# Moving the residual of two row blocks from TensorE to VectorE, and reordering the steps around it, in a fused retention and Fourier-mixing kernel

## The chip, the cores and the metric

The kernel runs on one core of a Trainium2 chip. A core has five engines that run their own instruction streams side by side and wait for one another through semaphores: TensorE (PE in the profile) multiplies matrices, VectorE (DVE) and ScalarE (ACT) do elementwise work and read TensorE's results out of PSUM, GpSimd (POOL) does elementwise work in SBUF and issues some transfers, and SyncE (SP) issues the other transfers. The metric is the device time of one execution in microseconds. Before the change it was 242.21 us, the median of three runs that lay between 242.1 and 242.36.

## The reference

The first half is retention, a linear attention with a decaying state, for 4 batches, 8 heads, 768 positions and head size 64. The second half adds a two-dimensional Fourier transform of the result to it, normalises each row and adds a two-layer network:

```python
for t in range(S):
    state = gamma[None, :, None, None] * state + np.einsum('bhd,bhe->bhde', k[:, :, t], v[:, :, t])
    y[:, :, t] = scale * np.einsum('bhd,bhde->bhe', q[:, :, t], state)
x = y.transpose(0, 2, 1, 3).reshape(B, S, H * D)
X = np.fft.fft(np.fft.fft(x, axis=1), axis=2)
u = x + np.real(X)
un = (u - u.mean(-1)) / np.sqrt(u.var(-1) + 1e-06)
out = u + np.maximum(un @ w_ch1, 0.0) @ w_ch2
```

The weights w_ch1 and w_ch2 have 512 x 2048 and 2048 x 512 elements. Inputs and output are float32.

## The kernel before, in words

The 768 rows of a batch are six chunks of 128 rows. Retention works on pairs of heads, four to a batch. For each pair q, k and v are loaded, cast to 16 bits (q16, kd, v16) and transposed on TensorE; TensorE then makes the scores of a chunk (wkA), VectorE masks and scales them (atm), TensorE makes the chunk states (wkK), VectorE scans them over the chunks (s), and TensorE adds up the output from both (wkY). ScalarE or VectorE evicts wkY into x, the input of the Fourier part.

The Fourier transform is done as matrix products with tables of cosines and sines: csp and ssp over the positions, cd and sd over the 512 columns. VectorE first folds x onto its sums and differences (xab), a DFT over positions gives g, and a second product with cd and sd gives pq. For column zero there is a small product with csn, a copy of the cosine table in another order, whose results become the per-row number g0. Row blocks 0 to 2 come straight from g; blocks 3 to 5 use a mirrored copy, g16r. Then u is the residual x plus pq plus g0, statistics of u follow (bst, stats), un is u minus its mean in 16 bits, and unT its transpose. The first layer makes psh from unT and the weight w116 (L1104 in batch 0), ht is its evicted positive part, the second layer makes psc from ht and w216 (L1130), and ob is the output.

The four batches are chained in software: while the network of batch b runs on TensorE, the retention of batch b + 1 is mixed in. Batch 0 has nothing before it, so its retention and its Fourier part are a start-up phase written out by hand: the string FIRST names every step in the order in which it is issued, and the function pin ties the steps of each engine to that order. Each engine runs its own steps in that order and waits where an input is missing. After FIRST the function emit sorts the remaining steps by due times, and behind those a scheduler may still move instructions of an engine past each other.

The names in FIRST that matter here have a step, numbers, and an engine after the @ sign (a ScalarE, v VectorE, g GpSimd). For pair i: am i h is the score product of half h (the function am_unit, L522), ae the mask (L536), kv the chunk states (L550), sc the scan (L559), yi and yx the output products (L572, L582), x the eviction (L599 on VectorE, L596 on ScalarE), fs the fold (L760), xs a row sum for the mean (L805). s e c d is a part of the first DFT (L827; e says cosine or sine, c the column half, d the side), and ge its eviction (L837). g0, g1 and g2 are three parts of the column-zero step: a small copy and scaling on VectorE (L874, L882), nine small TensorE products (L891), and two small VectorE steps (L897, L900). sa b p is part p of the second product of block b (L921): part 1 is the residual, two products of an identity with x. ua is the step that writes u (L929, L931), bn its statistics (L953, L954), nh and n write un (L943, L963), pt and pe transpose and evict block 0's un (L975, L981), gr copies one of the four mirrored tables (L863), w issues a weight transfer, csn copies a third of the reordered table (L355).

PSUM results live in rotating buffers: five banks for the products of the start-up (ps_g), and three (ps_pm) for psh and psc. A product that takes a bank waits until its former content has been evicted. In batch 0 the first layer goes block by block: for each of blocks 0, 1 and 2 there are four groups of 16 products (the function h0_unit), evicted in turn by ScalarE (groups 0 and 2, L1111) and VectorE (groups 1 and 3, L1113). Between the last n step and these evictions ScalarE also makes eight mask copies (late_consts, L277), which are tied behind the last n. The mirrored products for blocks 3 to 5 (L1025, L1028) are mixed in between.

The q, k and v of batch 0 are loaded by SP at the start (L215). Two q loads of batch 1 follow directly on SP (L220, L221, issued at L195). The eight weight transfers are issued by GpSimd at their w steps. The next SP loads wait for the seventh weight transfer.

Of the kernel before, what the change touches and what calls it, by code (L numbers as in the profile page):

```python
# [12 lines left out]
ALU = mybir.AluOpType  # L13
# [26 lines left out]
v22@a s010 k30@a t30 e30@a t31 v21@g e31@a ae201@v ta30 ae200@v kv2 ae211@v yi21 ae210@v gk2@g  # L40
sc2 csn2@a w1 csn1@v am30 ae300@v ta31 yi20 yx2 v32@g x20@a ae301@v xs0@v x21@a ta41 fl3@a gk3@g
s100 am31 ae311@v s000 v31@g kv3 fs2 s101 ge10@a ae310@v w2 s001 w3 yi31 sc3 ge00@a yi30 yx3 g0
x30@a sa00 sa10 edge x31@v fs3 w4 gr0 sa11 csn0@v s011 xs2@a xs3@v w5 s111 xs1@a sa20 mean
ge01@a sa02 sa01 ge11@v sa03 nh0@a gr3 sa12 nh1@a gr1 sa13 g1 sa21 pt0 g2 ua1@v pt1 sa22 pe0@a
pe1@a w6 ua0@v bn1 sa23 ua2@a gr2 n1 bn2 n2 w7
"""
# [15 lines left out]
def kernel(  # L62
# [122 lines left out]
    def load_unit(b, i, after=None, names="qkv"):  # L185
        def run():
            h0 = 2 * PAIR_ORDER[i]
            for name in names:
# [7 lines left out]
                if after is not None:  # L196
                    for x in (w_dma[after].ins, lb[0]["mm"].ins):
                        tc.add_manual_dep(dma.ins, x.name,
                                          mybir.DependencyInfo(mybir.DependencyClass.Sync,
                                                               mybir.DependencyReason.DATA),  # L200
                                          reason="loads in turn")
# [16 lines left out]
    for name, i in LOADS0:  # L218
        first_load(name, i, nc.sync)()
    load_unit(1, 0, None, "q")()  # L220
    load_unit(1, 1, None, "q")()  # L221

# [680 lines left out]

    lb = {}

    def sa_unit(kb, part):
        def run():
            if part == 0:
                if 0 not in lb:
                    lb[0] = dict(u=up.tile([P, NCH, DM], f32, tag="u32", name="u32"),  # L910
                                 unT=up.tile([P, 4, S], f16, tag="unT", name="unT"),
                                 st=stt.tile([P, NCH, 4], f32, tag="stats", name="stats"))
                lb[0]["pq", kb] = ps_g.tile([P, DM], f32, tag="g", name="pq0")
# [11 lines left out]
    def ua_unit(kb, eng):  # L925
        def run():
            dst, src, g0 = lb[0]["u"][:, kb], lb[0]["pq", kb], fd[0]["g0"][:, kb:kb + 1]
            if eng == "a":
                nc.scalar.activation(dst, src, AF.Identity, bias=g0, scale=1.0)  # L929
            else:  # L930
                nc.vector.tensor_scalar(out=dst, in0=src, scalar1=g0, scalar2=0.0, op0=ALU.add,  # L931
                                        op1=ALU.add)
        return run
# [162 lines left out]

    def h0_unit(kb, g):
        def run():
            unT = lb[0]["unT"]
            psh = ps_pm.tile([P, 4, P], f32, tag="pm", name="psh0")  # L1100
            for f in range(4):
                fb = 4 * g + f
                for cb in range(4):
                    mm = nc.tensor.matmul(psh[:, f], w116[:, cb, fb * P:(fb + 1) * P],  # L1104
                                          unT[:, cb, kb * P:(kb + 1) * P],
                                          start=(cb == 0), stop=(cb == 3))
# [81 lines left out]
    def first_unit(name):  # L1188
# [17 lines left out]
        if kind == "ge":  # L1206
            return s1e_unit(n[0], n[1], eng or "a")
        if kind == "nh":
            return n0_unit(n[0], eng or "a")
# [34 lines left out]
    def mix_units(b, kbs, s0, s1, u0, u1):  # L1244
        def turn(j):
            def run():
# [6 lines left out]
                ([unT_unit(b, kb) for kb in kbs], u0, u1)]  # L1253

    def emit(streams):
        ev = []
# [19 lines left out]
    for b in range(B):  # L1276
        majors = []
        if b == 0:
            for kb in range(3):
                if kb:  # L1280
                    majors.append(unT_unit(0, kb))
                majors += [h0_unit(kb, g) for g in range(4)]
        else:
            majors += [h_unit(b, 0, fb) for fb in range(NFB)]
# [57 lines left out]
```

## Time and profile before

The profiled execution took 242.18 us, against a median of 242.21; its span, from the first to the last instruction, was 240.4 us.

| Engine | Busy us | Share of the span |
|---|---|---|
| PE (TensorE matmul) | 228.3 | 95% |
| DVE (VectorE) | 173.4 | 72% |
| PE weight loads | 142.5 | 59% |
| ACT (ScalarE) | 120.8 | 50% |
| POOL (GpSimd) | 82.8 | 34% |

The granted TensorE clock was 1.0 over the span. The chain of work that ended last is 85% TensorE, 4% VectorE, 3% transfers. In a row of a timeline the first number is the start in microseconds from the beginning of the span and the second the time from the first start to the last end in that row; then come the engine, the line, the operation, the result and its inputs, the shape, the count, and in brackets the idle time before it with what ended it. Matmuls overlap, so the work of one is better read from the distance between two starts than from its duration.

### The profile page before, as it was taken

The numbers are of one execution on the slowest core, as the hardware profiler recorded it, in microseconds if no ns is written. First come the engines' busy times: TensorE is split into PE (matmuls) and PEld (weight loads), VectorE is DVE, ScalarE is ACT, GpSimd is POOL, SyncE is SP. The second block draws the span as 40 slices with busy tenths as digits, with TensorE's granted clock in tenths as the row PEclk, the third lists the DMA queues.
The fourth block names the chain that finished last, engine by engine and source line by source line (L and its number), as shares of the span: only waits on it lengthen the run. The fifth ranks groups of instructions, "written<-read, shape, count | busy, mean of one in ns | idle before, by whom it ended". The sixth has DMA issues, their size and how long they took to land.

```text
span 240.4 us, 5243 instructions
## 1 busy us (share of the span) xinstructions
PE 228.3 (95%) x1999; PEld 142.5 (59%) x1999; DVE 173.4 (72%) x421; ACT 120.8 (50%) x268; POOL 82.8 (34%) x151
## 2 busy tenths in 40 slices
PE   0988999999999999999999999999999999999994
PEld 0466779766774756665567446655675455446542
DVE  8999887958898789977895749977886557215121
ACT  5989758675864544931148406722366227203400
POOL 7678802675300197840002808920004124000000
PEclk9999999999999999999999999999999999999999
DMA  7999999999999289979999488675100331221012
GB/s 181 231 271 238 236 206 208 215 248 246 260 215 230 47 197 218 179 144 146 256 277 208 103 174 213 131 109 153 46 0 0 90 109 24 43 90 45 0 44 87
DMA packets 100808, 36.77 MB, mean 153 GB/s; under 512 B 91440, under 2 KB 97840, under 8 KB 100784
## 3 DMA queue, kind: packets, MB, share of 16 engines
q1 hardware_dynamic: 96560, 32.25, 63.2%
q0 software_dynamic: 4224, 4.19, 10.5%
q8 instruction: 15, 0.25, 0.5%
q14 instruction: 9, 0.07, 0.1%
HBM read 27.26 MB, written 6.29 MB: 140 GB/s over the span
## 4 chain that ended last, share of the span: by engine, by line
PE 85%; DVE 4%; DMA 3%; POOL 2%; ACT 2%; SPq 1%; issue 1%; ACTq 0%
PE psc L1130 34%; PE psh L1087 28%; PE psh L1104 3%; PE wkA L664 3%; DMA v<-in_v_dram 3%; PE ps L847 3%; PE wkY L718 2%; PE pq L1009 2%; PE ps L827 1%; PE wkY L714 1%; PE wkK L683 1%; PE pq L921 1%; SPq L215 1%; PE tq L620 1%; POOL q16z L453 1%
## 5 line engine op out<-in xcount | busy, mean ns | idle before, releaser
L1130 PE MATMUL psc<-w,ht 128*128 128x512 f16 (+2 forms) x400 | 88.9, 370 | 0.0
L1087 PE MATMUL psh<-unT,w 128*128 128x384 f16 x448 | 81.6, 326 | 0.3 <-ACT ht L1091 0.3
L1130 PEld LDWEIGHTS <-ht 128*128 128x128 f16 x400 | 37.6, 98 | 36.7
L1087 PEld LDWEIGHTS <-w 128*128 128x128 f16 x448 | 42.1, 98 | 24.2 <-issue 0.8
L1091 ACT ACTIVATE ht<-psh 128x384 f16<-128x384 f32 x66 | 31.7, 490 | 41.2 <-PE psh L1087 40.6
L1037 POOL TENSOR_TENSOR u<-u,x 128x256 f32<-128x256 f32 x21 | 13.3, 635 | 107.8 <-DVE u L1016 95.6
L1134 DVE SCALAR_TENSOR_TENSOR ob<-psc,stats,u 128x512 f32<-128x512 f32 (+2 forms) x25 | 18.1, 725 | 29.2 <-PE psc L1130 29.0
L1093 DVE TENSOR_SCALAR ht<-psh 128x384 f16<-128x384 f32 x46 | 25.3, 550 | 8.9 <-PE psh L1087 8.4
L667 DVE TENSOR_TENSOR atm<-wkA,maskp 128x512 f16<-128x512 f32 x36 | 23.6, 681 | 1.5 <-PE wkA L664 1.5
L1051 ACT ACTIVATE un<-u,stats 128x512 f16<-128x512 f32 x21 | 14.9, 719 | 12.2 <-DVE stats L1050 8.2
L1049 DVE BATCH_NORM_STATS2 bst<-u 128x6 f32<-128x512 f32 x21 | 14.5, 688 | 4.9 <-POOL u L1039 4.7
L693 DVE SCALAR_TENSOR_TENSOR s<-s,gk,wkK 128x128 f16<-128x128 f16 x48 | 16.2, 337 | 2.4 <-ACT s L689 1.6
L726 ACT ACTIVATE x<-wkY,gexp 128x384 f16<-128x384 f32 x24 | 12.9, 581 | 9.0 <-PE wkY L718 8.9
L438 POOL TENSOR_SCALAR kd<-k,gexp 128x384 f16<-128x384 f32 x24 | 13.8, 586 | 3.3 <-DMA k<-in_k_dram 3.1
L664 PE MATMUL wkA<-qTz,kT 128*128 128x256 f16 x72 | 13.2, 272 | 0.1
L1039 POOL TENSOR_TENSOR u<-u,x 128x256 f32<-128x256 f32 x21 | 13.3, 635 | 0.0
L1011 ACT COPY qn<-pq 128x128 f32<-128x128 f32 x18 | 4.9, 274 | 13.7 <-PE pq L1009 13.7
L1104 PEld LDWEIGHTS <-w 128*128 128x128 f16 x192 | 11.0, 98 | 0.9 <-issue 0.6
L1104 PE MATMUL psh<-unT,w 128*128 128x128 f16 x192 | 11.4, 219 | 0.1
L1016 DVE SCALAR_TENSOR_TENSOR u<-pq,g,qn 128x256 f32<-128x256 f32 x18 | 8.5, 474 | 3.2 <-PE psh L1087 2.5
L443 POOL TENSOR_SCALAR v<-v 128x768 f16<-128x768 f32 x12 | 10.0, 832 | 1.6 <-DMA v<-in_v_dram 1.6
L664 PEld LDWEIGHTS <-kT 128*128 128x128 f16 x72 | 6.9, 98 | 5.7 <-issue 0.6
(177 smaller groups left out, 311.9 us busy)
## 6 DMA issues: line engine op xcount, KB each, us to landing
q<-in_q_dram SPq DMA_DIRECT2D x16, 384.0 KB, 6.1
k<-in_k_dram SPq DMA_DIRECT2D x16, 384.0 KB, 5.4
v<-in_v_dram SPq DMA_DIRECT2D x16, 384.0 KB, 6.0
out_dram<-ob SPq DMA_DIRECT2D x23, 256.0 KB, 2.4
w<-in_moe_w_ch_dram POOLq DMA_DIRECT2D x8, 512.0 KB, 10.9
unT<-un SPq DMA_TRANSPOSE x15, 2.4
out_dram<-ob SPq DMA_DIRECT2D x1, 192.0 KB, 1.9
kT<-kd SPq DMA_TRANSPOSE x10, 3.0
```

What stands on the lines that cost most here:

```text
L438: kc = nc.gpsimd.tensor_scalar(out=kd[:, :, h2, :], in0=k32[:, h2], scalar1=gkd[:, h0 + h2:h0 + h2 + 1], scalar2=1.0, op0=ALU.mult, op1=AL ...
L664: mm = nc.tensor.matmul(wk[:, c2], st["kT"][:, c, :], st["qT"][:, :, c, :], start=True, stop=True)
L667: nc.vector.tensor_tensor(out=st["atm"][:, 2 * part:2 * part + 2], in0=wk, in1=maskp[:, PAIR_ORDER[i]].unsqueeze(1).to_broadcast([P, 2, 2, ...
L693: nc.vector.scalar_tensor_tensor(out=s16[:, c], in0=s16[:, c - 1], scalar=gk2[:, hp:hp + 1], in1=wk[:, c - c0], op0=ALU.mult, op1=ALU.add)
L1049: nc.vector.bn_stats(bst, u[:, kb, :])
L1051: nc.scalar.activation(un, u[:, kb, :], AF.Identity, bias=stats[:, kb, 0:1], scale=-1.0)
L1087: nc.tensor.matmul(psh, w116[:, cb, fb * P:(fb + 1) * P], unT[:, cb, rt * 384:(rt + 1) * 384], start=(cb == 0), stop=(cb == 3))
L1091: nc.scalar.activation(ht16[:, fb, :], psh, AF.Relu, bias=0.0, scale=-1.0)
L1093: nc.vector.tensor_scalar(out=ht16[:, fb, :], in0=psh, scalar1=-1.0, scalar2=0.0, op0=ALU.mult, op1=ALU.max)
L1104: mm = nc.tensor.matmul(psh[:, f], w116[:, cb, fb * P:(fb + 1) * P], unT[:, cb, kb * P:(kb + 1) * P], start=(cb == 0), stop=(cb == 3))
L1130: nc.tensor.matmul(psc[:, c0:c1], ht16[:, fb, rb3 * P:(rb3 + 1) * P], w216[:, fb, c0:c1], start=(fb == 0), stop=(fb == NFB - 1))
L1134: nc.vector.scalar_tensor_tensor(out=ob[:, c0:c1], in0=psc[:, c0:c1], scalar=lb[b]["st"][:, rb, 3:4], in1=lb[b]["u"][:, rb, c0:c1], op0=AL ...
```

## The change

In the order string, two table copies (csn1, csn0) move from the middle of the fourth pair's attention to behind its scan, and the row sum xs0 moves from there to behind the last fold. The DFT part s100 moves ahead of am30. The small product g1 moves ahead of edge, g2 behind ge11. The residual parts sa11 and sa21 of blocks 1 and 2 are taken out; in their place ua for blocks 1 and 2 adds x on VectorE in two instructions of 256 columns each, which take the PSUM product, g0 and x together. Block 2's u moves from ScalarE to VectorE and block 0's u from VectorE to ScalarE. The four mirrored copies gr move behind bn2. For GpSimd, the table step gk3 moves behind v31.

The two early q loads are no longer issued at the start: two new steps, lq02 and lq13, issue them with a wait for the third and the fourth weight transfer. In the function h0_unit the transposes of the next block's un are now issued in the middle of the last group of a block, and an empty step (done) takes their old place, so that the due times of all others stay as they were.

```diff
@@ FIRST
-sc2 csn2@a w1 csn1@v am30 ae300@v ta31 yi20 yx2 v32@g x20@a ae301@v xs0@v x21@a ta41 fl3@a gk3@g
-s100 am31 ae311@v s000 v31@g kv3 fs2 s101 ge10@a ae310@v w2 s001 w3 yi31 sc3 ge00@a yi30 yx3 g0
-x30@a sa00 sa10 edge x31@v fs3 w4 gr0 sa11 csn0@v s011 xs2@a xs3@v w5 s111 xs1@a sa20 mean
-ge01@a sa02 sa01 ge11@v sa03 nh0@a gr3 sa12 nh1@a gr1 sa13 g1 sa21 pt0 g2 ua1@v pt1 sa22 pe0@a
-pe1@a w6 ua0@v bn1 sa23 ua2@a gr2 n1 bn2 n2 w7
+sc2 csn2@a w1 s100 am30 ae300@v ta31 yi20 yx2 v32@g x20@a ae301@v x21@a ta41 fl3@a am31 ae311@v
+s000 v31@g gk3@g kv3 fs2 s101 ge10@a ae310@v w2 s001 w3 lq02 yi31 sc3 csn1@v ge00@a yi30 csn0@v
+yx3 g0 x30@a sa00 sa10 g1 edge x31@v fs3 xs0@v w4 lq13 s011 xs2@a xs3@v w5 s111 xs1@a sa20 mean
+ge01@a sa02 sa01 ge11@v g2 sa03 sa12 sa13 ua1@v bn1 nh0@a nh1@a pt0 pt1 sa22 pe0@a pe1@a n1 w6
+ua0@a sa23 ua2@v bn2 gr3 gr1 gr0 gr2 n2 w7
@@ load_unit
-                    for x in (w_dma[after].ins, lb[0]["mm"].ins):
+                    for x in [w_dma[after].ins] + ([lb[0]["mm"].ins] if "mm" in lb[0] else []):
@@ start of the kernel
-    load_unit(1, 0, None, "q")()
-    load_unit(1, 1, None, "q")()
@@ ua_unit
-            if eng == "a":
+            if kb:
+                x = xts[0][:, kb]
+                for c0, r in ((0, x[:, 0, 1:257]), (256, x[:, 1, 257:1:-1])):
+                    nc.vector.scalar_tensor_tensor(out=dst[:, c0:c0 + 256],
+                                                   in0=src[:, c0:c0 + 256], scalar=g0, in1=r,
+                                                   op0=ALU.add, op1=ALU.add)
+            elif eng == "a":
                 nc.scalar.activation(dst, src, AF.Identity, bias=g0, scale=1.0)
@@ h0_unit
-    def h0_unit(kb, g):
+    def h0_unit(kb, g, between=None):
...
                 fb = 4 * g + f
+                if f == 2 and between:
+                    between()
@@ first_unit
+        if kind == "lq":
+            return load_unit(1, n[0], n[1], "q")
@@ the majors of batch 0
-                if kb:
-                    majors.append(unT_unit(0, kb))
-                majors += [h0_unit(kb, g) for g in range(4)]
+                majors += [h0_unit(kb, g, unT_unit(0, kb + 1) if kb < 2 and g == 3 else None)
+                           for g in range(4)] + [done] * (kb < 2)
```

More of the change, by code (lines that the diff above doesn't have):

```diff
@@ L902, in g0_c @@
         fd[b]["g0"] = g0.rearrange("p a k -> p (a k)")
-    lb = {}
+    lb = {0: {}}
     def sa_unit(kb, part):
@@ L908, in run @@
             if part == 0:
-                if 0 not in lb:
-                    lb[0] = dict(u=up.tile([P, NCH, DM], f32, tag="u32", name="u32"),
+                if "u" not in lb[0]:
+                    lb[0].update(u=up.tile([P, NCH, DM], f32, tag="u32", name="u32"),
                                  unT=up.tile([P, 4, S], f16, tag="unT", name="unT"),
@@ L1253, in mix_units, with done @@
                 ([unT_unit(b, kb) for kb in kbs], u0, u1)]
+    def done():
+        pass
     def emit(streams):
```

## The prediction

> **What bounds the kernel now.** I read the page's busy shares first, then TensorE in order of time through the stretch that the diff rewrites (about 21 to 46 us), then VectorE, ScalarE and the weight transfers over the same stretch.
>
> ```profile
> span 240.4 us, 5243 instructions
> ...
> PE 228.3 (95%) x1999; PEld 142.5 (59%) x1999; DVE 173.4 (72%) x421; ACT 120.8 (50%) x268; POOL 82.8 (34%) x151
> ```
>
> TensorE is the bound: 95% of the span. Busy time hides short stalls, since matmuls overlap, so I go by the distance from one start to the next. These are TensorE's rows in order of time, where the fourth pair's attention ends (start, duration, line, result, count):
>
> ```profile
> 21.75 0.35 PE L572 MATMUL wkY<-v,atm 128*128 128x64 f16 x6
> 22.28 0.34 PE L522 MATMUL wkA<-qTz,kT 64*128 64x128 f16 x6 [0.18 <-ACT kT L508]
> ...
> 22.84 0.53 PE L582 MATMUL wkY<-s,qTz 64*128 64x64 f16 x10
> 23.29 0.69 PE L827 MATMUL ps<-ssp,xab 128*128 128x193 f16 x6
> 23.91 0.39 PE L522 MATMUL wkA<-qTz,kT 64*128 64x128 f16 x6
> ...
> 28.06 0.38 PE L921 MATMUL pq<-x,ident 128*128 128x256 f16 x2
> 28.46 0.70 PE L827 MATMUL ps<-csp,xab 128*128 128x193 f16 x6
> ```
>
> VectorE in the same stretch, with later rows whose prices I need:
>
> ```profile
> 22.66 0.36 DVE L355 COPY csn<-csp 128x384 f16<-128x384 f16 x1
> 22.91 1.02 DVE L536 SCALAR_TENSOR_TENSOR atm<-wkA,maskf 128x384 f16<-128x384 f32 x2
> 23.84 0.28 DVE L805 TENSOR_REDUCE xm<-x 128x1 f32<-128x128 f16 x1
> ...
> 25.82 0.81 DVE L559 TENSOR_TENSOR_SCAN s<-gk,wkK 128x320 f16<-128x320 f32 x1
> 26.55 0.14 DVE L874 COPY xg<-xab 128x6 f16<-128x6 f16 x1
> 26.73 0.23 DVE L882 TENSOR_SCALAR xg<-xg,sgn 128x6 f16<-128x6 f16 x1
> 27.33 0.62 DVE L599 TENSOR_SCALAR x<-wkY,gexp 128x384 f16<-128x384 f32 x1 [0.37 <-PE wkY L582]
> 28.05 0.63 DVE L760 TENSOR_TENSOR xab<-x 128x384 f16<-128x384 f16 x2
> 28.59 0.37 DVE L863 COPY g16r<-g 128x384 f16<-128x384 f16 x1
> ...
> 31.90 1.41 DVE L931 TENSOR_SCALAR u<-pq,g 128x512 f32<-128x512 f32 x2
> 33.23 0.68 DVE L953 BATCH_NORM_STATS2 bst<-u 128x6 f32<-128x512 f32 x1
> 33.95 0.18 DVE L954 BATCH_NORM_AGGREGATE stats<-bst 128x2 f32<-128x6 f32 x1
> 34.05 0.23 DVE L863 COPY g16r<-g 128x384 f16<-128x384 f16 x1
> 34.19 0.69 DVE L953 BATCH_NORM_STATS2 bst<-u 128x6 f32<-128x512 f32 x1
> ...
> 41.42 0.47 DVE L1033 SCALAR_TENSOR_TENSOR u<-pq,g,qn 128x255 f32<-128x255 f32 x1
> ```
>
> TensorE where the first layer of the network (L1104) begins, up to the second layer (L1130), and ScalarE beside it:
>
> ```profile
> 31.09 0.37 PE L891 MATMUL ps<-xg,csn 128*128 128x4 f16 x9
> 31.32 0.38 PE L921 MATMUL pq<-x,ident 128*128 128x256 f16 x2
> 31.54 0.50 PE L975 MATMUL pst<-ident,un 128*128 128x128 f16 x4
> ...
> 32.50 3.00 PE L1104 MATMUL psh<-unT,w 128*128 128x128 f16 x48
> ...
> 35.72 1.05 PE L1104 MATMUL psh<-unT,w 128*128 128x128 f16 x16
> ...
> 38.35 7.31 PE L1104 MATMUL psh<-unT,w 128*128 128x128 f16 x128
> 45.49 2.75 PE L1130 MATMUL psc<-w,ht 128*128 128x512 f16 x12
> ```
>
> ```profile
> 30.86 0.84 ACT L943 ACTIVATE un<-pq,mu 128x256 f16<-128x256 f32 x2 [1.06 <-DVE g16r L863]
> ...
> 35.50 0.72 ACT L963 ACTIVATE un<-u,stats 128x512 f16<-128x512 f32 x1 [0.61 <-DVE stats L954]
> 36.13 1.69 ACT L277 ACTIVATE maskp<-maskf 128x128 f32<-128x128 f32 x8
> 37.72 1.06 ACT L1111 ACTIVATE ht<-psh 128x512 f16<-128x512 f32 x2
> ```
>
> The reader is to see a relay between 23 and 38 us: TensorE products, a VectorE or ScalarE step, the next products. TensorE's own work fills nearly all of it, but each start hangs on a step elsewhere.
>
> **The change, part by part.** Times are the profiled execution's; "to 22.66" means my time for the changed kernel.
>
> *What leaves TensorE.* Two residual products for each of two row blocks, four of 256 columns. A pair holds TensorE from 31.32 to 31.54, 0.22 us; two pairs 0.44 us. This is the whole direct gain, an upper bound unless stalls shrink too.
>
> *One fold group ahead (s100 before am30).* Before, TensorE waits 0.18 us for kT and am30 starts at 22.28. Now the six s100 products (23.29 to 23.91, 0.62) follow yi21, whose six I take at 0.29 us: am30 starts at 21.75 + 0.29 + 0.62 = 22.66. It and yi20 take 0.56 (22.28 to 22.84), yx2 0.45, so TensorE reaches am31 at 23.67. But am31 reuses the banks of am30, which VectorE must mask first. VectorE begins when am30 ends (22.66 + 0.34, then 0.02), 23.02, and needs 1.02: done at 24.04. So am31 is in effect 0.18 late against 23.91, and s100, which covered this wait before, is spent. I carry +0.18 on TensorE.
>
> *Table copies and row sum.* Two csn copies and one row sum leave the first half of VectorE's stretch. csn starts at 22.66 and the mask behind it at 22.91, 0.25 us; the row sum costs 0.28. In their old place they now save nothing, as VectorE waits there for am30. They return behind the fourth pair's scan, ahead of the last x eviction (L599). The scan moves from 25.82 to 25.96 (its masks and folds start 0.14 later). The scan holds VectorE for 0.73 (25.82 to 26.55), the copies for 0.25 each, the two small xg steps until 0.41 after their start (26.55 to 26.73 + 0.23): L599 starts at 27.6, where it started at 27.33 after an idle 0.37. So the copies use up that idle time and 0.25 more. The fold behind it starts at 28.30 and TensorE's s011 at 28.71, not 28.46. The row sum goes behind the fold, where VectorE next waits for TensorE: nothing, or 0.28 if that cover goes.
>
> *Residual of block 1, and the small product g1.* TensorE is 0.18 late at the residual's place, which ran from 28.06 to 28.28 before waiting for the fold. The residual goes, g1 (31.09 to 31.32, 0.23) comes: TensorE is ready at 28.47 and waits 0.24 for the fold. The first 0.22 us saved thus becomes a longer wait.
>
> *Residual of block 2.* From s011 the stretch to the last product of block 0 is unchanged but for its order and starts 0.25 late; about 0.05 of that is an old gap that closes. nh0 on ScalarE thus starts at 31.05 instead of 30.86 and its halves end at 31.5 and 31.9. TensorE, without g1 and without the second residual, is at the transposes by 31.27 and waits for both halves. The two products that follow still hide the eviction of the transposes, and L1104 starts at 32.70, not 32.50. So the second 0.22 and g1's 0.23 go into waiting for nh0.
>
> *Residual on VectorE.* In place of one 512-element step per block (1.41 for two, now one of them from ScalarE) come two of 256 with three operands, priced by the nearest form, 0.47 each and 0.39 from start to start: 0.87 a block. Bounds are 0.70 (half of 1.41) and 0.94 (no overlap). The sum: block 1's pair starts at 31.47, its statistics take 0.9 (33.23 to 33.95 + 0.18), block 2's pair 0.87, its statistics 0.9; un of block 2 on ScalarE starts at 35.1, not 35.50: 0.4 earlier. With it the eight mask copies (36.13) move 0.4 earlier, and the first ScalarE eviction of L1104 from 37.72 to 37.31.
>
> *Mirrored copies behind the statistics.* Four g16r copies now stand together ahead of the first VectorE eviction of L1104, which frees the bank that block 0's last 16 products need (35.72). At 0.17 each (between the 0.14 and the 0.23 of the row at 34.05, the copy that stands nearest in time) that eviction ends at 36.31 and the products start at 36.36. At 0.37 each, the row at 28.59, it is 0.8 later (a rival).
>
> *Transposes of un put inside the last group.* In the changed order both blocks' eight transposes precede that group; only two of the six mirrored product pairs (0.11 a product) do. TensorE has done group, transposes and eight of those twelve products by 37.7 and then waits for the bank of block 0's first group, evicted from 37.31 in 0.63: block 1 starts at 37.94, 0.41 earlier than 38.35, but with four sd and two cd products, 0.65 us, still to come. L1130 starts at 37.94 + 7.14 + 0.65 = 45.73, not 45.49: **+0.24**.
>
> *Early q.* Two q loads now wait for the third and fourth weight transfers. On SP nothing else is ready: the k load behind them waits for the seventh. The later weight transfers:
>
> ```profile
> L1151 POOL DMA_DIRECT2D w<-in_moe_w_ch_dram x4: 760/775/790, 25.9 to 28.1; - x4
> DMA to landing us min/median/max: 11.7/14.5/17.2
> ```
>
> They land from 25.9 + 11.7 = 37.6 to 28.1 + 17.2 = 45.3 us, one in 2.6. The last is needed behind the 12 products of the row at 45.49, so after 48.2. The two q loads (768 KB) are worth 3.8 us at that pace. Whatever they take from the later weights they first gave back to the earlier ones, so I take nothing; the low bound is no gain, as no TensorE wait on a weight shows; the high bound is 45.3 + 3.8 = 49.1, a wait of 0.6 us. The Trainium skill ("DMA: Bandwidth & Descriptors", section on queues, rings and completion order) states that each engine takes turns between its queues, packet by packet. By that rule the q loads take a share from the later weights and the last could be late, the fourth rival below. No wait here can show it, as both kinds have landed before they are wanted.
>
> *After 46 us.* Four of the six mirrored product pairs come later, by up to some 4 us for the last (0.65 us of them behind five groups of 0.9), and with them VectorE's and Pool's work for blocks 3 to 5. Its results go into the second half of the network (L1087), far behind the first, so I take nothing. Between 62 and 79 us the two orders differ again. There TensorE meets a wait that VectorE sets:
>
> ```profile
> 77.99 0.38 PE L891 MATMUL ps<-xg,csn 128*128 128x4 f16 x9 [0.15 <-DVE xg L882]
> ```
>
> I price that stretch at nothing, within -0.3 to +0.3, from a few waits of this size.
>
> **Sum.** 242.18 (span 240.4 and 1.78 around it; the median of the runs, 242.21, is the same) + 0.24 = **242.4 us**. The saved 0.44 is spent in three waits that move onto steps of VectorE and ScalarE.
>
> **The rivals.**
> 1. TensorE stays the bound and the relay has more slack than I see: 0.44 off, and of the old short waits (0.18 at 22.28, 0.18 before 28.46) some go: 241.4 to 241.8. For: 95% busy. Against: the moved copies sit on L599, which had only 0.37 idle.
> 2. Slower: the four mirrored copies. If they cost 0.37 each, the VectorE eviction starts at 36.4, block 0's last group at 37.15, block 1 at about 38.5, L1130 at 46.3: +0.8, 243.0. It decides as soon as the eviction starts later than about 35.9, when the bank of block 1 no longer hides it. For: 28.59 shows 0.37. Against: that row ran while Pool was issuing.
> 3. The change does nothing, because the reordered stretch to 79 us gives back the 0.24: 242.2.
> 4. The last weight is late: 242.4 + 0.6 = 243.0. Against: bytes before it are the same.
>
> **How the numbers follow.** The forecast 0.47, rival 1 0.19, rival 2 0.15, rival 3 0.12, rival 4 0.07. About 0.2% (0.5 us) is what a measurement of this kernel can tell from no change. Forecast and rival 3 lie inside it, save some 0.06 of the forecast where its bounds add up above 242.7; of rival 1, 0.16 lies below 241.7 and 0.03 inside; rivals 2 and 4 lie above with their 0.22. That makes faster 0.16, same 0.56 and slower 0.28. The range runs from rival 1 to rivals 2 and 4: 241.5 to 243.1.
>
> **What would show it.** Right: L599's last x eviction has no idle before it and starts near 27.6; TensorE waits some 0.2 us before s011 and before the transposes of block 0; un of block 2 starts near 35.1; block 1 of L1104 near 37.9 behind a ScalarE eviction; L1130 near 45.7. Wrong: L1104 starting before 32.4 (rival 1), the first VectorE eviction of L1104 starting after 36 (rival 2), a TensorE wait on w after 48 (rival 4), or a second wait near 78 us that grew or vanished. The forecast fails if the two halves of the residual take another time than 0.87 a block, for the statistics, the second un and the mask copies all stand behind them.

## The result, and the profile after

The changed kernel takes 242.69 us (median of 22 runs, 242.27 to 243.78), the kernel before 242.22 in 22 runs beside it (241.89 to 243.14). The ratio is 1.0023, with a 95% interval of 1.0014 to 1.0031: slower by 0.34 to 0.75 us. The forecast was 242.4, in the range of 241.5 to 243.1. So the direction of the sum was right and its size was half of what came; the section on the prediction shows that the direction owes something to luck.

The first lines of the changed kernel's page, whose profiled execution took 242.64 us:

```profile
span 240.8 us, 5237 instructions
...
PE 227.0 (94%) x1995; PEld 142.1 (59%) x1995; DVE 173.8 (72%) x423; ACT 120.2 (50%) x268; POOL 82.8 (34%) x151
```

TensorE is busy for 1.3 us less (228.3 before) in a span that is 0.4 longer. By the distance between starts the four products that left were worth 0.44; what left TensorE became waiting. TensorE in order of time, from the fourth pair's attention to the second layer; lines of the file have shifted by a few, L1104 and L1130 of the first and second layer are now L1110 and L1136:

```profile
20.97 0.51 PE L494 MATMUL tq<-ident,kd 128*128 128x128 f16 x6 [0.44 <-POOL kd L465]
...
22.64 0.34 PE L520 MATMUL wkA<-qTz,kT 64*128 64x128 f16 x6
...
24.09 0.32 PE L520 MATMUL wkA<-qTz,kT 64*128 64x128 f16 x5 [0.25 <-DVE atm L534]
...
28.94 0.70 PE L825 MATMUL ps<-csp,xab 128*128 128x193 f16 x6 [0.38 <-DVE xab L758]
...
31.79 0.65 PE L979 MATMUL pst<-ident,un 128*128 128x128 f16 x4
...
32.90 3.00 PE L1110 MATMUL psh<-unT,w 128*128 128x128 f16 x48
...
36.53 1.05 PE L1110 MATMUL psh<-unT,w 128*128 128x128 f16 x16
...
38.10 4.63 PE L1110 MATMUL psh<-unT,w 128*128 128x128 f16 x80
...
46.03 2.75 PE L1136 MATMUL psc<-w,ht 128*128 128x512 f16 x12
```

ScalarE beside it, with the first two evictions of the first layer (L1117), and later the last of these evictions behind un of a mirrored block (L1055):

```profile
37.48 1.05 ACT L1117 ACTIVATE ht<-psh 128x512 f16<-128x512 f32 x2
...
44.77 0.72 ACT L1055 ACTIVATE un<-u,stats 128x512 f16<-128x512 f32 x1 [0.87 <-DVE stats L1054]
45.40 0.58 ACT L1117 ACTIVATE ht<-psh 128x512 f16<-128x512 f32 x1
```

Beside TensorE's rows of before one sees the cosine fold group (28.46 before) 0.48 later, the first layer (32.50) 0.40, the second layer (45.49) 0.54. Executions of one kernel differ at the start, so each has to be measured from a point ahead of the change: the transposes at 20.97 stood at 20.88 before, so 0.09 of every difference is not the change's. That leaves 0.45 us by the second layer.

VectorE of the changed kernel, where the moved copies stand:

```profile
25.93 0.81 DVE L557 TENSOR_TENSOR_SCAN s<-gk,wkK 128x320 f16<-128x320 f32 x1
26.66 0.71 DVE L353 COPY csn<-csp 128x384 f16<-128x384 f16 x2
27.26 0.38 DVE L872 COPY xg<-xab 128x6 f16<-128x6 f16 x1
27.67 0.23 DVE L880 TENSOR_SCALAR xg<-xg,sgn 128x6 f16<-128x6 f16 x1
27.81 0.61 DVE L597 TENSOR_SCALAR x<-wkY,gexp 128x384 f16<-128x384 f32 x1
```

There is no idle time from the scan to the last x eviction, and the two copies and the two small steps hold VectorE for 1.15 us (26.66 to 27.81).

Later on two waits decide. SP's queue before and after, first the k load of batch 1, then the transfers that transpose k:

```profile
42.86 0.37 SPq L195 DMA_DIRECT2D k<-in_k_dram  x1
...
60.65 2.73 SPq L616 DMA_TRANSPOSE kT<-kd  x2
```

```profile
31.57 2.91 SPq L195 DMA_DIRECT2D q<-in_q_dram  x2
44.43 0.37 SPq L195 DMA_DIRECT2D k<-in_k_dram  x1
...
62.29 2.74 SPq L614 DMA_TRANSPOSE kT<-kd  x2
```

And TensorE at 66 and at 116 us, before and after:

```profile
65.86 0.82 PE L664 MATMUL wkA<-qTz,kT 128*128 128x256 f16 x6
...
69.58 0.38 PE L664 MATMUL wkA<-qTz,kT 128*128 128x256 f16 x2
...
113.27 2.75 PE L1130 MATMUL psc<-w,ht 128*128 128x512 f16 x12
116.16 0.38 PE L664 MATMUL wkA<-qTz,kT 128*128 128x256 f16 x2
```

```profile
66.19 0.83 PE L662 MATMUL wkA<-qTz,kT 128*128 128x256 f16 x6 [0.28 <-DMA kT<-kd]
...
70.38 0.38 PE L662 MATMUL wkA<-qTz,kT 128*128 128x256 f16 x2
...
114.02 2.75 PE L1136 MATMUL psc<-w,ht 128*128 128x512 f16 x12
116.61 0.38 PE L662 MATMUL wkA<-qTz,kT 128*128 128x256 f16 x2
```

At 66 us the changed kernel waits 0.28 for the transposed k. At 116 us it is the kernel before that stands still: its twelve products from 113.27 to the next start take 2.89 us, the same twelve after 114.02 take 2.59. That gap of 0.30 is gone, and with it 0.30 of the delay. The account of the profiled pair is thus: 0.09 (start) + 0.45 (up to the second layer) + 0.26 (at 66 us: 0.54 becomes 0.80 at 69.58) - 0.35 (from there to behind the gap at 116.16, 0.30 of it in the gap) = 0.45, the longer span to its rounding.

### The profile page after: what moved, and what is told of

It is laid out like the page before. It is cut to its first block, busy times and chain, and to the rows that moved or that the text cites. A ratio compares the mean times of both kernels' runs of the same rounds, so it can differ in the third digit from the quotient of the medians.

```text
span 240.8 us, 5237 instructions
## 1 busy us (share of the span) xinstructions
PE 227.0 (94%) x1995; PEld 142.1 (59%) x1995; DVE 173.8 (72%) x423; ACT 120.2 (50%) x268; POOL 82.8 (34%) x151
## 3 DMA queue, kind: packets, MB, share of 16 engines
HBM read 27.26 MB, written 6.29 MB: 139 GB/s over the span
## 4 chain that ended last, share of the span: by engine, by line
PE 70%; DMA 9%; DVE 9%; ACT 4%; POOL 3%; issue 2%; SPq 1%; ACTq 0%; POOLq 0%; DVEq 0%
PE psc L1136 29%; PE psh L1091 25%; DMA v<-in_v_dram 3%; PE ps L845 3%; PE wkA L662 3%; DMA k<-in_k_dram 3%; DMA q<-in_q_dram 2%; DMA kT<-kd 2%; PE pq L1013 2%; PE psh L1110 2%; PE wkY L716 2%; DVE atm L534 1%; SPq L215 1%; PE wkY L712 1%; PE wkK L681 1%
## 5 line engine op out<-in xcount | busy, mean ns | idle before, releaser
L1136 PE MATMUL psc<-w,ht 128*128 128x512 f16 (+2 forms) x400 | 88.9, 370 | 0.0
L1136 PEld LDWEIGHTS <-ht 128*128 128x128 f16 x400 | 37.6, 98 | 36.9
L1055 ACT ACTIVATE un<-u,stats 128x512 f16<-128x512 f32 x21 | 14.9, 720 | 14.4 <-DVE stats L1054 10.4
L1053 DVE BATCH_NORM_STATS2 bst<-u 128x6 f32<-128x512 f32 x21 | 14.5, 689 | 5.1 <-POOL u L1043 4.8
L1110 PE MATMUL psh<-unT,w 128*128 128x128 f16 x192 | 11.5, 219 | 0.1
L1110 PEld LDWEIGHTS <-w 128*128 128x128 f16 x192 | 11.1, 98 | 0.9 <-issue 0.6
```

Source lines behind the costliest of these rows:

```text
L1053: nc.vector.bn_stats(bst, u[:, kb, :])
L1055: nc.scalar.activation(un, u[:, kb, :], AF.Identity, bias=stats[:, kb, 0:1], scale=-1.0)
L1136: nc.tensor.matmul(psc[:, c0:c1], ht16[:, fb, rb3 * P:(rb3 + 1) * P], w216[:, fb, c0:c1], start=(fb == 0), stop=(fb == NFB - 1))
```

## The experiments

Three theories went in. The relay theory: the loss comes from VectorE's added work ahead of the last x eviction. The residual theory: the three-operand steps on VectorE cost more than TensorE saves. The early-q theory: the later q loads push the loads behind them. After the first two groups of runs a fourth was added, slack: what is won or lost early is taken back at the waits for transposed q and k at 66 and 116 us.

All times are medians, with the ratio to the kernel before measured on the same chip (its medians were 242.3, 242.5 and 242.32 for runs 1 to 4, 5 to 8 and 9 to 12).

| Run | Time us | Ratio (95% interval) |
|---|---|---|
| 1 copies in VectorE's waits, early q | 243.25 | 1.0043 (1.0023 to 1.0062) |
| 2 s100 back | 242.77 | 1.0023 (1.0011 to 1.0035) |
| 3 q loads at the start | 242.33 | 1.0005 (0.9996 to 1.0013) |
| 4 before + residual on VectorE | 242.60 | 1.0013 (1.0004 to 1.0022) |
| 5 copies in VectorE's waits, q at the start | 242.37 | 0.9994 (0.9985 to 1.0002) |
| 6 as 5, masks later | 242.69 | 1.0015 (1.0002 to 1.0028) |
| 7 before + early q | 242.93 | 1.0027 (1.0006 to 1.0048) |
| 8 before, profiled again | 242.84 | one run |
| 9 before without the two residuals | 242.53 | 1.0007 (0.9997 to 1.0018) |
| 10 before + two filler products | 242.49 | 1.0010 (1.0001 to 1.0019) |
| 11 q at the start, csn on ScalarE | 242.84 | 1.0022 (1.0013 to 1.0030) |
| 12 changed kernel, csn on ScalarE | 243.01 | 1.0034 (1.0020 to 1.0048) |

The next table says where the profiled executions gained or lost: how much later the same products start than in the first profile of before, in us. The first column is the start-up's own scatter and has to be taken off the others; the others are the scores at 60.05, the scores at 69.58 behind the wait for k, the products at 90.12, the scores at 116.16 and the states at 156.77.

| Kernel | 20.88 | 60.05 | 69.58 | 90.12 | 116.16 | 156.77 |
|---|---|---|---|---|---|---|
| changed | 0.09 | 0.54 | 0.80 | 0.75 | 0.45 | 0.44 |
| run 2 | 0.15 | 0.68 | 1.85 | 1.80 | 1.50 | 1.50 |
| run 3 | 0.27 | 0.65 | 0.64 | 0.59 | 0.29 | 0.31 |
| run 4 | 0.15 | 0.43 | 0.43 | 0.37 | 0.07 | 0.07 |
| run 5 | 0.15 | 0.55 | 1.26 | 1.20 | 0.90 | 0.89 |
| run 6 | 0.14 | 0.90 | 1.00 | 0.79 | 1.73 | 1.73 |
| run 7 | 0.15 | 1.04 | 1.03 | 1.04 | 0.82 | 0.80 |
| run 8 | 0.10 | 0.21 | 0.20 | 0.19 | 0.41 | 0.43 |
| run 9 | 0.09 | 0.72 | 0.71 | 0.66 | 0.36 | 0.35 |
| run 10 | 0.11 | 0.44 | 0.43 | 0.43 | 0.13 | 0.16 |
| run 11 | 0.12 | 1.00 | 0.99 | 0.94 | 0.67 | 0.72 |
| run 12 | 0.06 | 0.93 | 1.45 | 1.40 | 1.10 | 1.09 |

**Run 1: the copies in VectorE's waits.**

```diff
-sc2 csn2@a w1 s100 am30 ae300@v ta31 ... sc3 csn1@v ge00@a yi30 csn0@v
+sc2 csn2@a w1 csn1@v s100 am30 ae300@v csn0@v ta31 ... sc3 ge00@a yi30
```

> The changed kernel with one edit: the two csn copies stand in the two waits that VectorE has for the attention products of the fourth pair (0.17 us before 23.01, 0.41 us before 24.45), not ahead of the last x eviction. Relay theory (the copies and the small xg steps, 0.4 us on the last x eviction, make up most of the loss): that eviction starts near 27.4 instead of 27.81, the cosine fold group near 28.5 instead of 28.94 with less than 0.1 us of waiting, L1110 near 32.45 instead of 32.90, L1136 near 45.6 instead of 46.03, time 242.25 to 242.35. Residual theory (the three-operand steps on VectorE are the loss): the wait only moves to the next step and the time stays at 242.7. Early-q theory (the later k and v loads are the loss): L1136 moves, the time does not, 242.7.

It took 243.25, more than any of the three theories said; its interval still overlaps that of the changed kernel, so that it is slower than that one is not shown. The one execution that was profiled took 604.69 us, with the network's products at 688 and 810 ns in the mean (326 and 370 in the kernel before), and says nothing of these steps. Runs 5 and 7 bear on the cause.

**Run 2: s100 back behind the first products of the fourth pair.**

```diff
-w1 s100 am30 ... fl3@a am31
+w1 am30 ... fl3@a s100 am31
```

> The changed kernel with one edit: the fold group s100 back behind the first attention products of the fourth pair, where it stood before. Relay theory: the 0.25 us wait of the second products (am31) for the mask goes, the masks on VectorE and the scan come some 0.1 earlier, but the copies still stand ahead of the last x eviction: L597 near 27.7, s011 near 28.8, L1136 near 45.9, time 242.5 to 242.6. Residual theory and early-q theory: 242.7.

No gain: 242.77, and the ratio of the changed kernel. In the profiled execution, one of the slowest (243.71), the wait of am31 is gone, but the fold group starts at 29.07, behind a longer copy (two copies from 26.66 to 27.39), and the wait at 66 us is larger:

```profile
67.25 0.83 PE L662 MATMUL wkA<-qTz,kT 128*128 128x256 f16 x6 [1.19 <-DMA kT<-kd]
```

So moving s100 is not where the loss is: what is won at am31 is lost again at the copies. The wait for k is 1.19 here and 0.28 in the changed kernel, whose loads go by the same steps; it differs between executions.

**Run 3: the q loads at the start again.**

```diff
+    load_unit(1, 0, None, "q")()
+    load_unit(1, 1, None, "q")()
-... w3 lq02 yi31 ... w4 lq13 s011
+... w3 yi31 ... w4 s011
```

> The changed kernel with one edit: the two q loads of batch 1 asked for at the start again, without the wait for a weight transfer. Relay theory: the loss up to 46 us stays (L1136 near 46.0), the k load of batch 1 returns from 44.4 to about 42.9 and the 0.28 us wait at 66 us for the transposed k goes: 242.4 to 242.7. Early-q theory: nearly all of the loss goes, 242.2. Residual theory: 242.7.

242.33, level with the kernel before, and the interval of the ratio just fails to meet that of the changed kernel: the early q steps are worth 0.18%, some 0.4 us, close to the early-q theory's 242.2. Up to 60 us nothing improves (0.65 less 0.27 at the start is 0.38, against 0.45), as the relay theory said. But the k load starts at 42.88 again, no wait stands at 66 us (0.64 at 69.58), and the gap at 116 us returns 0.30. The times also lie closer together, 242.25 to 242.56. Both theories had a part of it.

**Run 4: the residual alone.**

```diff
+            if kb: (the two three-operand steps of the change)
-... gr0 sa11 csn0@v ... g1 sa21 pt0 ... ua0@v bn1 sa23 ua2@a
+... gr0 csn0@v ... g1 pt0 ... ua0@a bn1 sa23 ua2@v
```

> The kernel before with one part of the change: the residual of the second and third row blocks on VectorE, with block 0's bias step on ScalarE in exchange; order, copies, fold groups and q loads as before. Relay theory: the wait of s011 for the fold takes up the first 0.22 us, the other 0.22 shows: L1110 of block 0 near 32.3 instead of 32.5, un of block 2 near 35.6, L1136 near 45.4 instead of 45.49, time 242.0 to 242.2. Residual theory: the VectorE steps push un of block 2, the mask copies and the ScalarE evictions back, L1136 near 46, 242.6 to 242.8. Early-q theory: 242.0 to 242.2 too.

242.60: no gain. The transposes of block 0 start at 31.46 (31.54 before, so 0.23 earlier beside the 0.15 of the start), but the last group of block 0 has a new wait for VectorE, and the second layer starts at 45.93:

```profile
36.17 1.05 PE L1110 MATMUL psh<-unT,w 128*128 128x128 f16 x16 [0.37 <-DVE ht L1119]
...
45.93 2.75 PE L1136 MATMUL psc<-w,ht 128*128 128x512 f16 x12
```

In this order the residual theory is right in its time, but not by the path that it named: un of block 2 starts at 35.58, no later than before with the start taken off. VectorE's steps delay VectorE's own first eviction (35.46, and 35.01 before). The changed kernel's order avoids that wait (its last group starts at 36.53 behind other work). At 156.77 run 4 is no later than before once its start is taken off; the rest of its time is lost behind 200 us, where a ScalarE step stands with no cause shown.

**Run 5: copies in VectorE's waits, q at the start.** The edits of runs 1 and 3 together.

> The changed kernel with two edits: q loads at the start again, and both csn copies in VectorE's two waits for the attention products of the fourth pair. To be read against the run with the q loads alone put back (242.33). Relay theory: without the copies ahead of the last x eviction the cosine fold group starts about 0.35 us earlier relative to the transposes at 20 us, and so does everything up to the second layer: 241.9 to 242.0. Rival (the end of the relay is set by the mask copies on ScalarE and the evictions of L1110, not by the fold): the earlier start is lost again before the second layer, 242.3.

242.37, level with before and with run 3: the relay theory's 0.35 us did not come. Against run 1 the q loads alone make 0.9 us by the times and 1.2 by the ratios, which were measured on two chips. VectorE and Pool in this kernel explain why the holes were no holes:

```profile
22.93 1.09 POOL L479 TENSOR_SCALAR v<-v 128x384 f16<-128x384 f32 x2 [0.39 <-DMA v<-in_v_dram]
...
23.55 0.71 DVE L355 COPY csn<-csp 128x384 f16<-128x384 f16 x1
23.97 0.54 POOL L271 COPY gk<-gk 128x256 f32<-128x256 f32 x1
```

The second copy takes 0.61 to the next start, not 0.25, while Pool casts v. The mask behind it comes late, and TensorE waits at am31 (0.55, ended by ScalarE's eviction of x) in place of the fold group. The profiled execution was the slowest of its runs (243.1); it also waits 0.73 at 66 us with a k load at 44.11, so that wait can appear without the early q steps.

**Run 6: the mask copies behind the first two ScalarE evictions of the first layer.**

```diff
-    late_consts()
-                           for g in range(4)] + [done] * (kb < 2)
+                           for g in range(4)] + [late_consts if kb == 0 else done] * (kb < 2)
```

> The run before this with one more edit: the eight mask copies (maskp, 1.69 us on ScalarE) behind the first two ScalarE evictions of L1110 instead of ahead of them. Relay theory: the wait of some 0.25 us between block 0's last products and block 1's goes, 0.2 to 0.3 us less than without the edit, 241.6 to 241.8. Rival: the bank is not what block 1 waits for, or the next eviction waits behind the masks instead: no gain.

242.69, 0.3 slower than run 5. The wait ahead of block 1 does go, but others open at the end of the first layer:

```profile
45.35 0.72 ACT L1057 ACTIVATE un<-u,stats 128x512 f16<-128x512 f32 x1 [1.65 <-DVE stats L1056]
...
46.13 0.40 PE L1080 MATMUL pst<-ident,un 128*128 128x128 f16 x4 [0.20 <-ACT un L1057]
46.61 3.61 PE L1138 MATMUL psc<-w,ht 128*128 128x512 f16 x16
```

Eighty products now run without a break from 36.53, but eleven of the twelve mirrored products come behind them (six of twelve in run 5). Their statistics on VectorE are late, ScalarE waits for these at un, and its last eviction starts at 45.98, 0.63 ahead of the second layer; the masks are long done by then (38.5). At 60.05 the delay is 0.90. In this profile TensorE also waits 1.08 us at 116 us for the transposed q.

**Run 7: early q alone.**

```diff
-    load_unit(1, 0, None, "q")()
-    load_unit(1, 1, None, "q")()
-... w3 yi31 ... fs3 w4 gr0
+... w3 lq02 yi31 ... fs3 w4 lq13 gr0
```

> The kernel before with one part of the change: the two q loads of batch 1 behind the third and fourth weight transfers, all else as before. Early-q theory: the last weights land later, the k load of batch 1 starts at 44.4 to 45.0 instead of 42.9, and TensorE waits 0.2 to 1.2 us for the transposed k at 66 us: 242.5 to 243.2, with a wide spread. Rival (the wait needs the later relay too, since Pool's casts stand behind it): no wait at 66 us, 242.2 to 242.3.

242.93, from 242.11 to 245.42: as slow and as scattered as the early-q theory said, though not for its reason in the execution that was profiled. TensorE has no wait at 66 us there. The loss stands at 24 us, on VectorE and Pool:

```profile
22.57 0.52 POOL L477 TENSOR_SCALAR v<-v 128x384 f16<-128x384 f32 x1
22.81 1.36 DVE L353 COPY csn<-csp 128x384 f16<-128x384 f16 x1
23.03 0.40 POOL L269 COPY gk<-gk 128x256 f32<-128x256 f32 x1
23.39 0.51 POOL L477 TENSOR_SCALAR v<-v 128x384 f16<-128x384 f32 x1
...
24.07 0.54 DVE L534 SCALAR_TENSOR_TENSOR atm<-wkA,maskf 128x384 f16<-128x384 f32 x1
```

With the q loads out of the way, v of the last pair lands earlier (22.28, and 22.93 and 23.33 in the two profiles of before), and Pool's casts no longer wait for it: in both profiles of before Pool is idle from about 22.4 until 23.02 or 23.42, and the same copy takes 0.25 to the next start. Pool's row in the first of them:

```profile
23.02 0.50 POOL L479 TENSOR_SCALAR v<-v 128x384 f16<-128x384 f32 x1 [0.64 <-DMA v<-in_v_dram]
```

In run 7 it takes 1.26, until Pool's three instructions are through. So the early q steps and the table copy at its old place do not go together in this execution; the change moves both.

**Run 8: the kernel before, profiled again.**

> The kernel before, unchanged, profiled a second time. In its first profile TensorE stands still for 0.3 us at 116 us without any wait that the trace names, and the changed kernel does not. If that gap belongs to the program, it is at the same products again; if it is chance, it is gone or elsewhere. Time 242.2 either way to within 0.3.

The gap is at the same products again, and this time the trace names it:

```profile
116.57 0.38 PE L664 MATMUL wkA<-qTz,kT 128*128 128x256 f16 x2 [0.35 <-DMA qTz<-q16z]
```

The trace's 0.35 counts from the end of the last product. From start to start, as above, the pause is 0.52 us here (113.46 to 116.57, less 2.59) and 0.30 in the first profile. So the wait for the transposed q of batch 2 is a real one, and it can take up a delay ahead of it: in the changed kernel and in runs 2, 3, 4, 5, 9, 10 and 12 some 0.3 us of the delay is gone behind it. It need not: this second execution reached the same products 0.19 late and then waited longer still, so the transfer was later too. That a gain ahead of it would be worth nothing follows only if the transfer stays where it is; no kernel here got there earlier than the first profile. The second profile also repeats the collision. First it, then the first profile of before, at the copy csn that follows the last fold:

```profile
26.30 2.98 POOL L1151 DMA_DIRECT2D w<-in_moe_w_ch_dram  x4
...
28.87 0.62 DVE L355 COPY csn<-csp 128x384 f16<-128x384 f16 x1
29.39 0.26 DVE L805 TENSOR_REDUCE xm<-x 128x1 f32<-128x128 f16 x1
```

```profile
28.09 0.79 POOL L1151 DMA_DIRECT2D w<-in_moe_w_ch_dram  x1
...
28.89 0.37 DVE L355 COPY csn<-csp 128x384 f16<-128x384 f16 x1
29.15 0.27 DVE L805 TENSOR_REDUCE xm<-x 128x1 f32<-128x128 f16 x1
```

Where Pool issues weight transfers until 29.28, the copy takes 0.52 to the next start; where Pool is done at 28.88, it takes 0.26.

**Run 9: the residual left out.**

```diff
-... gr0 sa11 csn0@v ... g1 sa21 pt0
+... gr0 csn0@v ... g1 pt0
```

> The kernel before without the residual products of the second and third row blocks and with nothing in their place (those two blocks of batch 0 then lack their residual): the most that the change could bring, 0.44 us of TensorE. Direct theory: all of it shows, 0.44 us under the kernel before. Relay theory: 0.22 goes into the wait of the cosine fold group for VectorE, the other 0.22 shows, 0.2 us under the kernel before. Slack theory (TensorE waits at 116 us for the transposed q of batch 2 anyway, 0.3 to 0.5 us in the two profiles of the kernel before, so that what is won earlier lengthens that wait): no gain, within 0.1 us of the kernel before.

Not faster: 242.53, an interval from 0.07 us below to 0.44 above. Even with nothing in its place, the removed work brings nothing that can be seen. ScalarE and TensorE show what takes it:

```profile
36.30 1.69 ACT L277 ACTIVATE maskp<-maskf 128x128 f32<-128x128 f32 x8
...
37.90 1.05 ACT L1111 ACTIVATE ht<-psh 128x512 f16<-128x512 f32 x2
38.52 0.66 PE L1104 MATMUL psh<-unT,w 128*128 128x128 f16 x9 [0.58 <-ACT ht L1111]
```

Block 1 cannot start before the first ScalarE eviction has freed its bank, 0.62 us after 37.90, and that eviction stands behind the statistics of block 2, un and the masks, none of which hang on TensorE's residual. In the kernel before the same sum is 37.72 + 0.63 = 38.35, the very start of block 1: TensorE was not the bound there, if only by 0.14 us, for its last mirrored pair starts at 37.99 and takes 0.22. The run is not a clean removal, though: five of the twelve mirrored products, which all stood ahead of block 1 before, now stand behind it (0.54 us), TensorE waits 0.58 for the bank in their place, and the second layer starts at 46.21, later than before.

**Run 10: two filler products.**

```diff
-... sa13 g1 sa21
+... sa13 fill2 g1 sa21
```

> The kernel before with two filler products of 512 columns (0.43 us of TensorE) ahead of the small product g1 at 31 us, where TensorE is busy without a wait. Slack theory: the second layer starts 0.4 later (near 45.9), but the wait at 116 us shrinks by 0.3 and the time rises by 0.1 us only. Relay theory without that slack: 0.43 us over the kernel before.

0.43 us of extra TensorE work cost 0.17 us (0.02 to 0.46 by the interval). In the profile, start taken off, 0.33 of it is left at 60.05 and 0.02 behind 116 us. The slack theory stands in the profile; the interval alone does not exclude the other (0.43). The filler reaches block 1 through the same chain: it delays g1, and so u, the statistics, un and the masks; the first ScalarE eviction starts at 38.16 and block 1 at 38.79. So TensorE's work directly ahead of g1 is on the chain. Of the two residuals one stood ahead of the wait for VectorE's fold and the other behind g1.

**Runs 11 and 12: the copies on ScalarE**, with the q loads at the start and with the early q steps.

```diff
-... sc3 csn1@v ge00@a yi30 csn0@v yx3 ... sa10 g1 edge ... s111 xs1@a sa20 ... ge11@v g2 sa03 sa12 sa13 ua1@v
+... sc3 ge00@a yi30 yx3 ... sa10 edge ... s111 xs1@a csn1@a csn0@a sa20 ... ge11@v sa03 sa12 sa13 g1 g2 ua1@v
```

> The changed kernel with the q loads at the start and both csn copies on ScalarE, in its 0.88 us wait before the last fold cast, the small product g1 back behind the pq products: no table copy on VectorE, so none can meet Pool there. Relay theory: last x eviction near 27.4 plus the offset at 20 us, fold group 0.4 earlier than with the q loads alone put back, second layer 0.3 to 0.4 earlier, time 241.95 to 242.05. Slack theory: the second layer is 0.3 to 0.4 earlier, but TensorE waits that much longer at 66 or 116 us, 242.2 to 242.35.

> The changed kernel with both csn copies on ScalarE as in the run before this, and the early q loads kept. Relay theory: 0.3 to 0.4 us less than the changed kernel, 242.3 to 242.4. Slack theory: the wait for the transposed k at 66 us, which hangs on the loads, grows by what is won, 242.6 to 242.7.

242.84 and 243.01, both slower than their pairs (242.33 and 242.69), though for run 12 the intervals overlap. Two things change at once here, the place of the copies and that of g1. The first half of the relay theory is right: with no table copy on VectorE the fold group starts at 28.62 and 28.56, the transposes of block 0 at 31.65 and 31.58. The second half is wrong. With g1 back behind the pq products, g0 is late, and u, the statistics and un of block 2 follow it. From run 11:

```profile
36.50 0.40 PE L1080 MATMUL pst<-ident,un 128*128 128x128 f16 x4 [0.51 <-ACT un L969]
...
38.57 4.63 PE L1112 MATMUL psh<-unT,w 128*128 128x128 f16 x80
...
46.49 2.75 PE L1138 MATMUL psc<-w,ht 128*128 128x512 f16 x12
```

Against run 3, with each start taken off, 0.28 us won at the fold group (28.62 and 29.05) are 0.50 us lost at the second layer (46.49 and 46.14). What sets block 1 is the chain from g0 over the statistics to ScalarE, not the fold.

## Why the prediction was right, and where that was luck

*The whole.* The sum put the loss, 0.24 us, into the relay up to the second layer. The relay did lose, 0.45 us there. But run 3 keeps the relay's loss and takes back the early q loads alone, and it is level with the kernel before (242.33): the wait at 116 us hides most of the relay's loss. What the time shows is mainly the step that the prediction priced at nothing. So the relay was read rightly, and the direction of the time came out right in part by luck.

*s100 ahead.* Right, and small: am30 at 22.64 (22.66 forecast), and am31 waits for the mask. It ends its wait at 24.09, 0.18 after 23.91 as forecast, but 0.09 of this is the start's offset.

*Table copies.* This term of the relay was mis-sized. It had the copies at 0.25 each and the small xg steps at 0.41. From nearly the same start they took 0.60 for the two and 0.55, 0.24 us more in all, and L597 started at 27.81, not 27.6. Both rows stand inside the stretch in which Pool issues weight transfers (25.39 to 28.41), and run 8 and run 7 show what such copies can cost beside Pool. The prediction met this in the 0.37 of the row at 28.59 and used it against the rival of the mirrored copies only; it belonged to this step. It also had one fact wrong, as has the section on the change: only csn1 left the middle of the fourth pair's attention; csn0 stood behind the last fold, at 28.89.

*Residual of blocks 1 and 2, g1.* Right in kind: the removed products became waits, 0.51 ahead of s011 (0.24 forecast; g1 starts at 28.20 and takes 0.23) and 0.30 ahead of the transposes, and L1110 started at 32.90 (32.70). Of this 0.20, 0.09 is the start's offset, and the rest is that of the copies, handed on.

*Residual on VectorE and the mirrored copies.* Right: 0.88 and 0.85 a block for the 0.87 taken, un of block 2 at 35.26 (35.1), four copies in 0.65 to the next start, the first VectorE eviction at 35.79, so rival 2 fell. Block 1 at 38.10 stands 0.62 behind ScalarE's eviction at 37.48, as the sum had it (37.94). Run 9 makes the point harder than the prediction did: block 1 was bound by ScalarE before the change too.

*The second layer.* 46.03, 0.45 later than before without the offset, where +0.24 was forecast. Of the 0.21 between them only 0.07 is left of the copies at block 1 (38.10 less 0.09, against 37.94). The other 0.14 comes behind block 1, where the sum had 7.14 + 0.65 and the trace has 7.93. ScalarE's rows above show why: its last eviction of the first layer stands at 45.40 directly behind un of a mirrored block, and L1136 starts 0.63 after it, the distance that block 1 keeps from its eviction. Before, that eviction ran at 44.80, ahead of un. In runs 2 to 6, 11 and 12 the second layer starts 0.62 or 0.63 behind this eviction too. The prediction had moved the mirrored products and, with them, their work on VectorE and Pool, and took nothing for it. No run moves this eviction alone, so the cause is read from the distances.

*Early q.* Priced at nothing, with a look at the weights only. Its argument was that the early weights gain what the late ones lose. They do: the first four land 7.1 us after their issue in the median (8.4 before), the last four 16.5 (14.5). The weights also come before they are wanted (no wait on w, rival 4 fell). But the loads behind the seventh weight were not followed: k from 42.86 to 44.43, the transposes of k from 60.65 to 62.29, TensorE waiting at 66 us. Run 3 prices the step at some 0.4 us. The Trainium skill ("DMA: Bandwidth & Descriptors", section on queues, rings and completion order), that the queues share an engine by turns, spoke against this step, and k starting 1.6 us later agrees with it. That the later start is all the sharing's is not shown: run 5 has 44.11 with the q loads at the start.

*After 46 us.* Nothing was taken, within 0.3 either way. The two terms were +0.26 at 66 us and -0.30 at 116 us, and that they nearly cancel is luck: the sum held because of it. The second, the wait for the transposed q of batch 2, hid over a third of the loss and was in the trace of before as a gap. The wait near 78 us, of which the prediction warned, went from 0.15 to 0.20 only.

*Rival 1*, that the removed 0.44 shows, is refuted by the time and by runs 4 and 9, with the reservation made at run 9; run 10 shows that other work of TensorE does count there. Rival 3, no change, lies outside the interval. No version here beats both kernels; run 5 (0.9985 to 1.0002) is level with before.

## What to carry to other kernels

An engine that is busy for 95% of the span need not be the bound at the place where its work is cut: look for the step that releases its next product, and add up that chain. Before a gain or loss early in a kernel is booked, look for the next place where the bound engine waits for a transfer, for that wait can take it back. A load that is moved on a queue is priced by the transfers behind it, not by its own. A product that is moved behind others takes its steps on the other engines with it, and these can stand ahead of an eviction.

## What the runs showed of the hardware

Small 16-bit copies on VectorE could take two to five times as long beside Pool: csn 0.25 to the next start with Pool idle, 0.52 while Pool issued transfers, 0.61 and 1.26 while Pool cast and copied. To stand beside an issue is not enough. The changed kernel's second csn copy starts at 27.00, 0.15 us into an issue, and takes 0.26. Its first xg copy starts at 27.26, 0.41 into the same issue, and takes 0.41, to the issue's end at 27.67. In the two profiles of before this xg copy takes 0.18 (26.55, at the end of an issue) and 0.44 (26.65, in the middle of one). The copies that were held beside an issue went on where it ended; those that began within the first 0.15 us of one passed. The Trainium skill ("SBUF — State Buffer", section on who interferes with whom) states that such copies and Pool share one port pair as an exclusive lock, where the one that comes second waits for the whole instruction of the other. The traces agree in the waiting, save that a copy waited through three Pool instructions in a row (22.57 to 23.90 in run 7) and that an issue held a copy only from some point on. No run changed Pool's work alone, so the cause is argued from the pairs of profiles, not isolated.

Kernels that moved the q loads also scattered more: 242.25 to 242.56 with the loads at the start in run 3, 242.11 to 245.42 with them late in run 7, 241.89 to 243.14 in the 22 runs of the kernel before. The wait for the transposed k was 0, 0.28, 0.54, 0.73 and 1.19 us in single executions, so one profile does not price such a wait.
